# A pre-norm transformer block on one core: one tile's statistics on ScalarE, softmax sums of two units in groups of four, and a new instruction order

## The chip, the core and the metric

The kernel runs on one core of one Trainium2 chip. The metric is the device time of one execution in microseconds, the median of three runs. The engines are named as the profile names them: PE (TensorE matmuls, with its weight loads as PEld), ACT (ScalarE), DVE (VectorE), POOL (GpSimd) and SP (the queue that issues the DMAs).

## The reference

One transformer block over 2048 tokens with 1024 channels, 32 heads of 32 channels and an inner FFN width of 3584, all tensors in bf16. There is no causal mask. The layer norms have no learned scale.

```
h  = x + attention(layernorm(x)) @ wo      # qkv = layernorm(x) @ wqkv, softmax(q k / sqrt(32)) v
h2 = h + gelu(layernorm(h) @ w1 + b1) @ w2 + b2     # gelu in its tanh form
```

## The kernel before

The 2048 tokens are cut into 16 tiles of 128 rows, or into 8 units of 256 queries. The 32 heads form 8 groups (`G`) of 4 heads; the four heads of a group use the four 32-row or 32-column strips of the PE array at once. A *job* is one unit and one group, written (unit, group); there are 64 jobs. A job has 8 *rounds*, and a round covers 256 keys.

A round of a job goes through these steps. `Att.qk` makes eight matmuls of scores on PE (line 1017) into two pairs of PSUM banks. Two ACT instructions of 1024 columns (line 1029) take the exponential and write it into a slot of the ring `PT` (nine rounds; while the lead runs, fourteen further slots named `PX`). `Job.pv` (line 1075) multiplies with V, and into the same bank, beside the result, `Job.den` (line 1115) adds the softmax's row sums with a matrix of ones. To make those sums cheaper for PE, DVE first adds pairs of blocks within a round (line 1092) into one of three `PS` buffers, and for units 0 to 5 adds two such results (line 1098) before `den` takes them; `direct` rounds skip DVE and go from `PT` to `den`. In a normal job round 7 is direct, rounds 0 to 5 are added in three groups of two, and round 6 stands by itself. In the first three jobs, (0,0), (1,0) and (2,0), all rounds are direct. `Job.finish` turns the sums into reciprocals on DVE and writes the normalised output `OT`.

PSUM banks 0 to 5 hold scores. Banks 6 and 7 are shared: a job's result takes one of them, and all background matmuls (projections, output projection `wo`, `ffn1`, `ffn2`) take the other, or whichever is free. A `Slot` is a claim on one of the two.

The work is staged as follows. The *lead* loads x, normalises tiles pair by pair (`lead_norm`, `layer_norm`), transposes each tile on PE (`tr_tile`, `transposes`; line 847 for tiles 0 and 1), copies it to `xnT`, and makes keys and queries of group 0 (`proj_half`) and V (`proj_v1`), so that the first exponentials can start early. `LEAD_ACT` names the tiles whose transposed copy ACT makes; DVE makes the others. A layer norm consists of two half statistics per tile (`half_stats`, line 746), an average (line 755), a conversion `mvb` (759), `tb` (760) and `mvr` (766), a power on POOL (767), a reciprocal (769) and the normalisation itself (772). The remaining projections follow as background work beside the jobs in the order of `ORDER`: (3,0), then groups 1 to 4, then groups 5 to 7, of units 0 and 1 (units 2 and 3 too for group 1). For units 2 and later, the queries are made as background work by `late_q` and pass through DRAM. From then on a unit's output projection, second layer norm and FFN are background work beside the exponentials of later units. Between the exponentials ACT computes the tanh of the gelu (line 1294). The last unit's FFN is the tail.

No instruction order is written by hand. The kernel's text builds a graph of tasks, and `Graph.schedule` plans it with a model of each engine's cost, choosing by priority. The result is five fixed queues, one for each engine. `PRIO_SHIFT` adds a correction to the priority of single tasks and `GROUP_SHIFT` to the place of groups of background matmuls. `PV_BEGIN` and `PV_MUST` say, for each job, at how many waiting rounds `pv` may begin and must run. While the planned time is below `LEAD_HOLD`, DVE may stay idle for a moment when a task with a better priority is about to become ready. `fill_gaps` puts small matmuls without a use (line 1566) into planned gaps of PE in the lead, between 9 and 52 us. The planner's `dma` sizes are costs, not bytes: the factors 2.7 and 3.9 only make the model's transfers longer.

Of the kernel before, what the change touches and what calls it, by code (L numbers as in the profile page):

```python
# [14 lines left out]
LEAD_HOLD = 12.0  # L15
# [52 lines left out]
class Graph:  # L68
# [267 lines left out]
    def emit(self, e, obj):  # L336
# [10 lines left out]
PV_BEGIN = "6776776766675567666685766867867747778757674686786668888633466636"  # L347
PV_MUST = "3743746633366637646276643332732244443446233432453524324325757663"
GROUP_SHIFT = (
        "0:94 1:-298 2:244 3:378 4:-5 5:90 7:79 11:-10 13:-14 15:41 16:-152 17:-8 18:115 19:-291 22:-138 "  # L350
        "25:-30 26:-23 27:-3 28:13 29:-4 34:-8 35:-139 38:16 39:136 40:60 42:2 44:-33 45:90 47:28 52:25 "
        "53:-212 55:-117 56:-80 57:-18 58:25 65:75 67:-10 68:-25 69:295 75:-177 76:-84 78:-19 85:160 86:90 "
        "87:-61 88:-205 89:-62 90:-416 91:-111 95:28 96:49 97:13 98:38 101:598 102:138 103:-16 106:-6 "
        "108:-15 114:-115 115:-169 117:-1 118:-114 119:22 120:-11 122:-107 123:280 125:65 126:-136 127:-18 "
        "128:-5 129:13 130:-12 135:28 136:-30 138:-1 143:1 144:-3 145:11 152:-33 153:-84 155:39 157:-26 "
        "158:-22 162:-30 163:-14 164:-1 165:6 168:-18 170:-24 171:-16 172:50 173:23 174:27 175:45 178:-26 "
        "179:156 180:32 181:-144 188:186 189:4 190:-165 192:-13 193:-61 194:192 195:-16 196:-17 197:-25 "
        "198:-4 199:-219 200:185 203:97 204:-306 205:-31 206:-17 207:48 208:361 218:110 219:-26 220:13 "
        "221:159 222:157 223:361 225:139 226:-173 227:3 233:-18 235:-12 239:-88 248:-125 250:19 251:-159 "
        "253:-3 254:-45 259:-2 261:-24 262:-184 263:-41 268:16 278:-28 280:-84 281:6 283:82 284:79 285:551 "  # L360
        "286:-39 288:-29 289:-87 291:-294 292:274 294:-11 295:83 296:-16 298:246 299:62 310:50 312:14 "
        "315:-100 316:-14 319:7 321:74 322:-18 324:-34 325:-12 326:-214 329:-148 331:-205 332:-18 333:24 "
        "335:57 337:-94 ")
PRIO_SHIFT = (
        "0:-1 2:-2 3:-4 5:2 6:-2 7:-1 8:-15 9:-5 10:-1 13:-1 16:-1 17:4 53:-1 54:-2 57:-1 58:-1 59:2 62:-1 "
        "63:5 65:1 86:-1 87:1 121:2 122:-1 123:-1 124:-1 126:2 129:2 131:-1 132:-3 134:1 143:1 153:-2 154:-2 "
        "183:-3 185:1 186:1 187:-1 189:-1 191:-2 194:-7 195:-1 196:1 216:2 219:-3 222:3 224:-2 225:-1 252:2 "
        "253:1 254:-3 255:4 258:1 259:-4 260:1 261:1 262:-2 263:1 273:1 283:1 288:3 290:-1 293:1 294:5 317:2 "
        "318:-1 319:-1 321:1 322:-1 326:1 327:1 328:1 339:2 350:1 351:2 356:-1 357:-6 374:-2 378:-1 381:1 "
        "382:-1 383:1 384:1 385:2 386:-1 396:1 411:1 412:1 415:3 432:1 433:-1 434:-1 435:2 440:8 441:-2 "  # L370
        "443:-1 454:-1 465:-4 466:-1 469:3 471:-2 472:-1 489:1 495:1 497:-5 498:1 499:1 500:2 501:-2 511:2 "
        "521:-1 529:-1 547:-2 549:-1 550:2 552:-1 579:-2 596:-8 613:2 630:1 647:-2 681:1 715:1 716:-1 717:1 "
        "718:-1 719:-1 721:-2 722:-1 741:3 761:-1 765:1 766:-3 768:-1 769:1 773:-1 774:2 777:-1 780:-2 781:1 "
        "783:-1 785:-3 786:-2 788:-2 789:1 794:1 797:3 799:-1 800:1 803:-1 808:1 817:1 818:2 820:-3 824:1 "
        "827:1 834:1 835:-1 844:6 871:-1 880:-3 922:-1 955:-1 988:-1 1038:-3 1055:3 1072:-1 1092:2 1094:-2 "
        "1095:-1 1099:-2 1100:-1 1102:-2 1103:1 1105:1 1106:1 1109:-1 1118:1 1123:-1 1124:2 1127:1 1129:-2 "
        "1130:-2 1138:-2 1140:-1 1143:-9 1144:1 1146:-2 1155:2 1157:-4 1161:-1 1163:-4 1169:-3 1175:-2 "
        "1176:-2 1179:-2 1182:2 1185:1 1190:-6 1191:-1 1192:-4 1193:-2 1199:2 1201:3 1203:-1 1204:1 1206:-2 "
        "1207:-1 1209:-2 1210:2 1215:1 1216:2 1218:-2 1221:-2 1222:1 1225:1 1227:-1 1228:1 1230:-1 1233:1 "
        "1234:2 1237:-1 1245:-1 1250:-4 1258:-3 1259:-1 1262:1 1267:-1 1268:1 1270:1 1271:-2 1273:-2 1289:-1 "  # L380
        "1306:-1 1315:-3 1324:-2 1359:3 1420:-1 1424:1 1482:-1 1490:-1 1491:3 1494:-1 1496:-1 1499:1 1500:-1 "
        "1510:-1 1511:-1 1541:-2 1593:2 1630:3 1632:-1 1633:2 1635:2 1638:2 1640:-3 1644:1 1647:1 1649:-2 "
        "1650:-1 1652:-1 1659:-2 1661:-3 1664:1 1671:-2 1675:-1 1677:1 1678:-1 1687:-1 1689:-1 1693:2 "
        "1695:-1 1696:-1 1704:3 1705:1 1707:-6 1708:-4 1711:1 1714:2 1716:-1 1719:1 1720:1 1727:-2 1730:-1 "
        "1731:-1 1740:-1 1776:1 1810:1 1846:-2 1852:-1 1855:6 1857:-1 1861:1 1864:-1 1869:2 1876:-2 1878:2 "
        "1879:5 1882:4 1884:-6 1885:-5 1888:1 1892:2 1893:1 1894:-1 1895:-2 1896:-2 1898:-2 1906:-1 1910:2 "
        "1921:1 1928:3 1931:2 1933:-2 1940:1 1944:-1 1945:1 1947:-1 1948:-1 1966:-1 1975:-2 1984:1 2027:-1 "
        "2063:-1 2066:-1 2067:1 2071:-1 2072:-1 2074:2 2075:2 2077:-2 2081:1 2083:-1 2087:1 2089:-2 2090:1 "
        "2095:-1 2096:1 2101:-1 2105:1 2111:1 2112:2 2122:2 2131:1 2140:2 2149:-1 2209:-1 2231:4 2234:1 "
        "2236:-1 2240:5 2242:1 2243:1 2246:-1 2248:-1 2252:-1 2254:-1 2258:-1 2260:-2 2263:2 2264:-1 2266:2 "  # L390
        "2267:2 2270:4 2275:1 2276:3 2278:-2 2287:-1 2314:1 2325:1 2326:4 2328:-1 2329:-1 2334:1 2336:-1 "
        "2345:2 2346:3 2348:1 2349:1 2351:1 2352:3 2355:1 2360:2 2361:-3 2363:1 2364:1 2371:1 2373:-2 2374:7 "
        "2375:-2 2377:-2 2378:-1 2381:1 2385:-2 2388:2 2391:-1 2395:-1 2397:-1 2400:-1 2412:3 2416:1 2419:-1 "
        "2424:1 2425:-3 2426:-1 2427:1 2429:-2 2430:-1 2432:-3 2433:1 2440:-2 2443:-1 2444:3 2447:2 2449:-1 "
        "2452:1 2453:1 2456:1 2464:-1 2465:3 2471:2 2477:1 2478:2 2484:-1 2485:1 2492:-1 2493:1 2499:1 "
        "2504:1 2505:1 2513:-1 2516:-1 2520:1 2523:1 2527:1 2531:1 2533:2 2554:1 2555:1 2565:-1 2575:3 "
        "2577:-1 2587:-2 2596:3 2597:-3 2599:2 2601:-1 2611:-1 2620:-1 2621:1 2639:1 2642:-1 2648:-1 2649:-1 "
        "2651:-2 2653:-1 2654:-1 2655:-1 2661:3 2662:-1 2674:-1 2683:1 2684:1 2695:1 2725:-1 2736:1 2746:1 "
        "2747:-1 2748:1 2765:1 2766:1 2784:1 2787:1 2788:-2 2790:-1 2807:-2 2832:1 2869:1 2871:-1 2872:-1 "
        "2912:-1 2954:-3 2955:1 2975:-1 2976:1 2994:-1 3040:1 3041:-1 3042:-1 3044:1 3045:1 3047:-1 3048:-1 "  # L400
        "3053:1 3056:-1 3059:2 3064:-1 3067:1 3068:-2 3074:1 3076:2 3077:3 3079:-1 3086:-1 3087:1 3089:1 "
        "3094:-2 3095:-2 3100:-1 3101:1 3106:1 3108:1 3115:-2 3130:-1 3140:1 3177:1 3180:-1 3183:1 3196:1 "
        "3203:-1 3206:1 3207:1 3209:1 3212:4 3215:2 3227:-1 3229:-2 3235:1 3236:-1 3238:-1 3245:-1 3249:2 "
        "3253:-2 3254:1 3255:-1 3256:1 3260:3 3264:-1 3271:1 3274:1 3276:-2 3279:-2 3283:1 3292:-2 3299:-1 "
        "3301:-1 3306:-1 3307:2 3309:1 3315:-1 3317:-1 3318:-1 3323:1 3324:1 3330:1 3333:-2 3335:-4 3336:1 "
        "3339:1 3341:-1 3342:-1 3344:-2 3356:-2 3361:-1 3364:3 3373:-2 3392:-4 3401:-4 3403:3 3404:-1 "
        "3405:-2 3406:1 3407:-2 3408:1 3410:1 3413:1 3414:-2 3415:-3 3416:1 3417:1 3418:4 3419:1 3422:1 "
        "3423:-1 3425:1 3426:2 3489:-2 3490:1 3497:-2 3526:3 3527:-4 3556:-1 3557:-1 3575:1 3593:-1 3594:1 "
        "3595:1 3600:1 3637:-5 3639:1 3640:-1 3642:1 3681:2 3683:3 3684:-1 3701:-1 3702:1 3721:-1 3722:3 "
        "3726:1 3761:-1 3762:1 3763:-1 3768:-1 3803:-1 3804:-2 3805:2 3807:-2 3808:-2 3809:1 3845:1 3846:-2 "  # L410
        "3849:1 3850:1 3851:1 3852:-1 3853:1 3863:-1 3873:3 3874:-1 3875:2 3885:-2 3895:1 3896:1 3915:-4 "
# [65 lines left out]
def build_kernel(nc, A_x, A_wqkv, A_wo, B_w1, B_b1, B_w2, B_b2, out):  # L477
# [267 lines left out]
    def half_stats(i, c, src, B_src, prio):  # L745
        return dve(lambda v: v.bn_stats(st_l[:, i, 6 * c:6 * c + 6], src), 0.6, reads=[B_src], writes=[B_stl[i][c]], prio=prio)

    def layer_norm(tiles, prio, norm="dve", quick=True, at=None):

        n = len(tiles)  # L750
        i = ln_slots(n) if at is None else at
# [902 lines left out]
```

## Time and profile before

| | us |
|---|---|
| median of three runs (1068.94 to 1070.45) | 1069.12 |
| the profiled execution | 1069.67 |
| its span, first to last instruction | 1067.9 |
| first exponential starts | 15.37 |
| last exponential ends | 1007.87 |
| PE busy | 1041.4 |
| ACT busy | 1010.0 |
| DVE busy | 837.0 |

The page gives each engine's busy time as a share of the span. The view of windows gives the same for any stretch of the span, so that a stage can be read by itself. The view of waits names what an engine waited for, and the chain of waits follows the last instruction back. The timeline lists instructions in order of time, with the idle time before an instruction in square brackets and what ended it. An exponential of 1024 columns is shown with 1.03 us alone, but follows the one before after about 0.92 us, since their ends overlap. The granted PE clock was 1.00 in nearly all of the span.

### The profile page before, as it was taken

The page shows a single profiled execution, that of the slowest core. Times are in us where ns is not written, and L with a number is a line of the kernel's source. Part 1 is how long each engine was busy: PE and PEld are TensorE (multiplying, and loading weights), DVE is VectorE, ACT ScalarE, POOL GpSimd, SP SyncE. Part 2 cuts the span into 40 slices and gives each one's busy share as a digit, 9 for nine tenths or more (in the row PEclk, how much of TensorE's full clock was granted, in tenths as well). Part 3 has the DMA queues.
Part 4 walks back from the last instruction along what each step waited for, and adds up shares of the span by engine and source line. Part 5 has one row for each costly group of instructions (what it writes and reads, how often), then busy time and mean ns, then how long its engine had stood idle before and what let it go on. Part 6 is the DMA issues. An engine that isn't in the chain of part 4 may idle for free.

```text
span 1067.9 us, 39400 instructions
## 1 busy us (share of the span) xinstructions
PE 1041.4 (98%) x17738; PEld 598.2 (56%) x17738; DVE 837.0 (78%) x1648; ACT 1010.0 (95%) x1118; POOL 18.2 (2%) x34
## 2 busy tenths in 40 slices
PE   8999999999999999999999999999999999899998
PEld 6756555654447546644565466446546744474483
DVE  8757777777888997998799989978887876797511
ACT  5999999999999999999999999999999999999850
POOL 1100000000000000000000000000000000000000
PEclk9999999999999999999999999999999999999999
DMA  7920012005568588647776686577667756887640
GB/s 211 267 50 3 2 42 62 2 2 160 182 164 245 154 199 258 182 148 222 211 219 176 175 254 192 161 243 212 179 173 225 216 172 211 229 236 245 191 150 21
DMA packets 280136, 177.40 MB, mean 166 GB/s; under 512 B 41632, under 2 KB 274848, under 8 KB 279584
## 3 DMA queue, kind: packets, MB, share of 16 engines
q1 hardware_dynamic: 279968, 174.89, 56.5%
q8 instruction: 139, 2.28, 0.9%
q14 instruction: 29, 0.24, 0.1%
HBM read 160.96 MB, written 10.22 MB: 160 GB/s over the span
## 4 chain that ended last, share of the span: by engine, by line
ACT 73%; PE 22%; DMA 3%; DVE 2%; issue 0%; SPq 0%; DVEq 0%
ACT PT L1029 67%; PE ps L698 7%; PE ps L701 5%; ACT tg L1294 4%; PE ps L695 3%; PE ps L1017 3%; PE ps L1075 2%; ACT PX L1029 2%; PE ps L1115 1%; DMA b1b<-in_B_b_dram 1%; DMA a_w1r<-in_B_w_dram 1%; DMA a_w2r<-in_B_w_dram 1%; DMA hnT<-a_xb 1%; DVE PS L1092 0%; DMA xrb<-in_A_x_dram 0%
## 5 line engine op out<-in xcount | busy, mean ns | idle before, releaser
L1029 ACT ACTIVATE PT<-ps 128x1024 bf16<-128x1024 f32 x996 | 928.0, 1201 | 4.7 <-PE ps L1017 4.5
L1092 DVE TENSOR_TENSOR PS<-PT 128x1024 bf16<-128x1024 bf16 x425 | 286.3, 685 | 90.0 <-ACT PT L1029 50.2
L1017 PE MATMUL ps<-QT,KT 32*128 32x256 bf16 x4096 | 204.3, 273 | 9.3 <-ACT PT L1029 5.5
L1075 PE MATMUL ps<-PT,V 128*32 128x256 bf16 x3984 | 162.8, 274 | 0.1
L1017 PEld LDWEIGHTS ps<-QT,KT 32*128 32x128 bf16 x4096 | 60.9, 92 | 171.8 <-ACT PT L1029 161.7
L698 PE MATMUL ps<-hnT,a_w1r 128*128 128x256 bf16 x1161 | 144.0, 273 | 2.7 <-DVE tg L1293 0.8
L698 PE MATMUL ps<-a_w2r,gT 128*128 128x512 bf16 x538 | 132.3, 380 | 0.3
L698 PEld LDWEIGHTS ps<-hnT,a_w1r 128*128 128x128 bf16 x1161 | 105.7, 98 | 35.2 <-issue 18.6
L1075 PEld LDWEIGHTS ps<-PT,V 128*32 128x32 bf16 x3984 | 101.2, 97 | 31.7 <-issue 9.1
L1098 DVE TENSOR_TENSOR PS<-PS 128x1024 bf16<-128x1024 bf16 x135 | 92.4, 685 | 2.2
L1115 PE MATMUL ps<-PS,ones 128*32 128x256 bf16 x1160 | 80.6, 275 | 0.6 <-DVE PS L1092 0.3
L698 PEld LDWEIGHTS ps<-a_w2r,gT 128*128 128x128 bf16 x538 | 46.7, 98 | 61.4 <-issue 15.8
L1271 DVE TENSOR_TENSOR gT<-ps,b1f 128x512 bf16<-128x512 f32 x98 | 66.9, 685 | 17.3 <-PE ps L698 9.6
L695 PE MATMUL ps<-a_w2r,gT 128*32 128x512 bf16 x984 | 72.7, 381 | 0.9 <-DMA a_w2r<-in_B_w_dram 0.8
L1294 ACT ACTIVATE tg<-tg 128x1024 bf16<-128x1024 bf16 x49 | 58.7, 1226 | 0.0
L695 PE MATMUL ps<-hnT,a_w1r 128*32 128x256 bf16 x1628 | 57.9, 274 | 0.1
L695 PEld LDWEIGHTS ps<-hnT,a_w1r 128*32 128x32 bf16 x1628 | 40.7, 96 | 9.3 <-issue 7.4
L698 PE MATMUL ps<-a_w1r,OT 128*128 128x512 bf16 x168 | 41.9, 380 | 1.5 <-issue 0.8
L698 PE MATMUL ps<-xnT,Wall 128*128 128x512 bf16 (+1 forms) x170 | 40.8, 366 | 0.2 <-DVE QT L879 0.2
L698 PE MATMUL ps<-Wall,xnT 128*128 128x256 bf16 x302 | 39.8, 274 | 0.1
L1115 PEld LDWEIGHTS ps<-PS,ones 128*32 128x32 bf16 x1160 | 31.2, 97 | 15.0 <-issue 5.7
L695 PE MATMUL ps<-xnT,Wall 128*32 128x512 bf16 x568 | 39.4, 381 | 0.0
(105 smaller groups left out, 985.2 us busy)
## 6 DMA issues: line engine op xcount, KB each, us to landing
a_w2r<-in_B_w_dram SPq DMA_DIRECT2D x105, 512.0 KB, 4.9
a_w1r<-in_B_w_dram SPq DMA_DIRECT2D x98, 512.0 KB, 4.7
a_w1r<-in_A_wo_dram SPq DMA_DIRECT2D x32, 512.0 KB, 4.6
b_w1r<-in_B_w_dram SPq DMA_DIRECT2D x14, 512.0 KB, 5.1
a_w1r<-in_A_wqkv_dram SPq DMA_DIRECT2D x11, 512.0 KB, 4.3
Wall<-in_A_wqkv_dram SPq DMA_DIRECT2D x16, 256.0 KB, 4.9
hch<-in_A_x_dram SPq DMA_DIRECT2D x16, 256.0 KB, 4.7
xrb<-in_A_x_dram SPq DMA_DIRECT2D x14, 256.0 KB, 4.4
```

The source lines that it names most:

```text
L695: fns.append(lambda p, j=j: p.matmul(psum[32 * j:32 * j + 32, bi(bank), c0:c1], lhsT[:, 32 * j:32 * j + 32], rhs, start=start, stop=stop, ...
L698: t.whole = lambda p: p.matmul(psum[:, bi(bank), c0:c1], lhsT, rhs, start=start, stop=stop, skip_group_check=True)
L701: t = pe(lambda p: p.matmul(psum[:, bi(bank), c0:c1], lhsT, rhs, start=start, stop=stop), occ, reads=reads, writes=[bb(bank)], mode="full" ...
L1017: return p.matmul(psum[:, 2 * us[h // 2] + h % 2, n * i:n * i + n], KT[32 * h:32 * h + 32, g, k0:k0 + P], QT[32 * h:32 * h + 32, qs, 0:n], ...
L1029: x = act(lambda a, u=u, k=k: a.activation(pt(s)[:, k, :, :], psum[:, 2 * u:2 * u + 2, :], ACT.Exp, bias=0.0, scale=SCALE), 1024, reads=[B ...
L1075: fns.append(lambda p, i=i, h=h: p.matmul(psum[32 * h:32 * h + 32, bi(bank), 0:nq], V[:, g, nk * r + i, 32 * h:32 * h + 32], pt(s)[:, h // ...
L1092: dve(lambda v: v.tensor_tensor(PS[:, n, :, :], pairs[:, :, 0:256], pairs[:, :, 256:512], ALU.add), c_dve(1024, 2), reads=[B_PT[2 * s], B_ ...
L1098: dve(lambda v: v.tensor_tensor(PS[:, n, :, :], PS[:, n, :, :], PS[:, m, :, :], ALU.add), c_dve(1024, 2), reads=[B_PS[n], B_PS[m]], writes ...
L1115: fns.append(lambda p, h=h, rhs=rhs, i=i: p.matmul(psum[32 * h:32 * h + 32, bi(bank), nq:2 * nq], ones32[:, :], rhs, start=False, stop=las ...
L1271: drop(dve(lambda v: v.tensor_tensor(gT[:, fc:fc + 2, cs], psum[:, bi(bank), 0:2 * n].rearrange("p (f c) -> p f c", f=2), b1f[:, fc:fc + 2 ...
L1294: act(lambda a: a.activation(t, t, ACT.Tanh, bias=0.0, scale=math.sqrt(2.0 / math.pi)), c, reads=B_t, writes=B_t, prio=-1)
```

## The change

Three things change together. First, in the lead, tile 2's mean and variance come from two ACT instructions with an accumulated sum (a copy, and a square with the negated mean as bias) and two small DVE instructions, in place of two half statistics and an average on DVE. Tile 3's transposed copy and the first query copy go from ACT to DVE; x of tile 3 is loaded ahead of the first weights; V's copy of group 0 gets a better priority; and the hold reaches to 48 us. Second, in the jobs of units 0 and 1 for groups 1 to 7 (14 jobs), all eight rounds go through DVE in two groups of four, and none is direct. Other jobs keep their form. Third, all four tables of the order are replaced, and `fill_gaps` sees the score banks as free from their first use on instead of from 20 us on.

```
-LEAD_HOLD = 12.0
+LEAD_HOLD = 48.0
...
-PV_BEGIN = "6776776766675567666685766867867747778757674686786668888633466636"
-PV_MUST = "3743746633366637646276643332732244443446233432453524324325757663"
+PV_BEGIN = "7466868666566663766578667587867347887757875567678767876564886785"
+PV_MUST = "6553264375657772234355742223743664642632354443335522323335343233"
...
+    def act_stats(j, x_ap, B_x, o_ap, B_o, prio):
+        act(lambda a: a.activation(o_ap, x_ap, ACT.Copy, accum_out=st_l[:, j, 0:1]), 1024,
+            reads=B_x, writes=[B_o, B_stl[j][0]], prio=-3)
+        dve(lambda v: v.tensor_scalar(mv_l[:, j, 0:1], st_l[:, j, 0:1], 1.0 / D, None, ALU.mult), 0.08,
+            reads=[B_stl[j][0]], writes=[B_mv[j]], prio=prio - 6)
+        act(lambda a: a.activation(o_ap, x_ap, ACT.Square, bias=mv_l[:, j, 0:1], scale=-1.0, accum_out=st_l[:, j, 6:7]), 1024,
+            ap_bias=True, reads=B_x + [B_mv[j]], writes=[B_o, B_stl[j][1]], prio=-3)
+        dve(lambda v: v.tensor_scalar(mv_l[:, j, 1:2], st_l[:, j, 6:7], 1.0 / D, None, ALU.mult), 0.08,
+            reads=[B_stl[j][1]], writes=[B_mv[j]], prio=prio)
...
         for k, (x_ap, B_x, o_ap, B_o) in enumerate(tiles):
+            if k in by_act:
+                act_stats(i + k, x_ap, B_x, o_ap, B_o, prio)
+                continue
...
-    LEAD_ACT = [0, 2, 3]
+    LEAD_ACT = [0,2]
     LEAD_DMA = 16
+    STAT_ACT = [2]
...
-                    reads=[bb(bank)], writes=wr, prio=-4 if g == 0 else 0)
+                    reads=[bb(bank)], writes=wr, prio=-21 if g == 0 else 0)
...
-    def QUAD(qb, g):
-        return qb < QA or g < QG
+    def EARLY(qb, g):
+        return g >= 1 and qb < 2
+
+    def SIZE(qb, g):
+        return 4 if EARLY(qb, g) else 2 if qb < QA or g < QG else 1
 
     def DIRECT(qb, g):
-        return 16 if g == 0 and qb < DLEAD else 1
+        return 16 if g == 0 and qb < DLEAD else 0 if EARLY(qb, g) else 1
...
-                if self.half is None and r + 1 < self.nr - self.direct and self.quad:
-                    self.half = n
-                elif self.half is not None:
-                    m, self.half = self.half, None
+                m, self.acc = self.acc, n
+                if m is not None:
                     dve(lambda v: v.tensor_tensor(PS[:, n, :, :], PS[:, n, :, :], PS[:, m, :, :], ALU.add), c_dve(1024, 2),
                         reads=[B_PS[n], B_PS[m]], writes=[B_PS[n]], prio=-2)
+                self.held += 1
+                if self.held == self.size or r + 1 == self.nr - self.direct:
                     self.sums.append((n, False))
-                else:
-                    self.sums.append((n, False))
+                    self.acc, self.held = None, 0
...
-    x_tile(0, -6, 2)
-    x_tile(1, -6, 2)
-    x_tile(2, -5)
-    load_w(WQ, -5, 0, P)
-    load_w(WK, -5, 0, P)
-    for tt in range(3, 8):
-        x_tile(tt, -5)
+    x_tile(0, -9, 2)
+    x_tile(1, -9, 2)
+    x_tile(2, -8)
+    x_tile(3, -8)
+    load_w(WQ, -7, 0, P)
+    load_w(WK, -7, 0, P)
+    for tt in range(4, 8):
+        x_tile(tt, -6)
     load_w(WV, -5, 0, 256)
...
         if hc == 0:
-            proj_half(0, 0, 0, ev)
+            proj_half(0, 0, 0, "dve")
...
-                held.setdefault(2 * u, [(0.0, t1 / 2.6, [])]).append((t.done - t.lat - t.occ, x.done, [x]))
+                held.setdefault(2 * u, [(0.0, x.done - 0.01, [])]).append((t.done - t.lat - t.occ, x.done, [x]))
```

Left out here are the two long tables `GROUP_SHIFT` and `PRIO_SHIFT` (all of their entries are new) and the planner's cost factors for the first transfers.

## The prediction

> **What bounds the kernel now.** First the page's busy shares with the chain of waits, then the windows, because shares average over stages with different limits.
>
> ```profile
> PE 1041.4 (98%) x17738; PEld 598.2 (56%) x17738; DVE 837.0 (78%) x1648; ACT 1010.0 (95%) x1118; POOL 18.2 (2%) x34
> ...
> ACT 73%; PE 22%; DMA 3%; DVE 2%; issue 0%; SPq 0%; DVEq 0%
> ```
>
> PE has the larger share and ACT the longer chain; the windows decide (columns: stretch, length, then busy us and count of PE, PEld, DVE, ACT, POOL; clock, DMA share, GB/s). I cut them at the first exp (15.37) and at the end of the last (1007.87).
>
> ```profile
> 15.37:60.00 44.63, 41.83 (x756) 31.03 (x757) 32.67 (x93) 43.36 (x51) 4.40 (x6) 1.00 0.83 232
> 60.00:100.00 40.00, 39.50 (x910) 25.69 (x902) 28.19 (x55) 39.59 (x44) 0.00 (x0) 1.00 0.01 3
> 100.00:310.00 210.00, 207.84 (x3683) 111.01 (x3679) 165.76 (x307) 209.50 (x230) 1.99 (x2) 1.00 0.25 74
> 250.00:310.00 60.00, 58.57 (x1113) 28.09 (x1101) 50.40 (x99) 60.00 (x67) 1.99 (x2) 1.00 0.66 192
> 1007.87:1015.20 7.33, 7.33 (x54) 3.51 (x54) 6.00 (x23) 2.68 (x5) 0.54 (x1) 1.00 0.98 300
> 1015.20:1067.90 52.70, 49.53 (x393) 33.90 (x391) 5.87 (x12) 15.13 (x31) 0.55 (x1) 0.99 0.26 82
> ```
>
> From first to last exp ACT idles 1.27 (to 60), 0.41 (to 100), 0.50 (to 310) and, in the same view cut further on, 1.39, 0.78, 0.05, 0 and 0.84: 5.24 us of 992.50. The span is thus 15.37 to the first exp, 987.26 of ACT work, 5.24 of ACT idle, and 60.03 behind the last exp, where the last unit's normalisation and FFN follow in a fixed order. PE is full as well, but a faster PE shortens nothing unless ACT was waiting for it; that is at most 5.24 us. So a gain has to come from an earlier first exp, from ACT work removed behind it, or from the 5.24.
>
> The timeline of the lead shows what stands before the first exp (start, duration, engine, line).
>
> ```profile
> 6.22 1.29 DVE L746 BATCH_NORM_STATS2 st<-xrb 128x6 f32<-128x512 bf16 x2
> 7.42 0.15 DVE L759 CAST mvb<-mv 128x4 bf16<-128x4 f32 x1
> ...
> 10.40 1.09 ACT L854 ACTIVATE xnT<-ps 128x512 bf16<-128x512 bf16 x2 [8.39 <-PE ps L847]
> 12.54 0.38 ACT L980 ACTIVATE QT<-ps 128x256 bf16<-128x256 f32 x1 [1.05 <-PE ps L701]
> 13.10 0.38 ACT L980 ACTIVATE KT<-ps 128x256 bf16<-128x256 f32 x1 [0.17 <-PE ps L701]
> 13.54 1.94 ACT L801 ACTIVATE xnT<-ps 128x1024 bf16<-128x1024 bf16 x2
> 15.37 1.03 ACT L1029 ACTIVATE PT<-ps 128x1024 bf16<-128x1024 f32 x1
> ```
>
> Tile 2's statistics sit on DVE between the averages of tiles 0 and 1 and their mvb, which starts the chain to the first normalised tile; ACT is idle 8.39 us meanwhile; and the first exp, whose scores were begun at 13.66, queues behind the two copies of tiles 2 and 3.
>
> **Part 1: the lead.** Tile 2's statistics leave DVE: two halves, 1.29 us, so mvb can start up to 1.3 us sooner. W is no barrier: the K weights were issued near 4.55 and land some 5.1 us later (DMA view), 9.7; K's matmuls start at 12.06 (half of the 2.00 us from 11.06) and would move to 10.8. In the new DMA order Q's weights go one transfer sooner, tile 2 one later: issued at about 2.9 plus 4.4, it lands near 7.3. On ACT come a Copy and a Square over 1024 columns. No such op with a sum is in the trace; the nearest row is the 1024-wide copy, 1.94 for two, so about 1.0 each, with a 0.15 us DVE op between and another behind (as mvb and tb). Bounds: 0.9 (an exp's spacing, 3.77 for four) and 1.4 (should the sum need another small op, like the smallest ACT copy, 0.38). They run about 7.3 to 9.5, inside ACT's idle stretch, but tile 0's copy, then wanted at 9.1, waits to 9.5: of the 1.3 us I keep 0.9. ACT loses tile 3's copy in front of the first exp: 0.97. The QT copy leaves ACT at 12.54, where it idled: 0, and on DVE (0.41) it is done before KT is. DVE loses 1.29 and an average (0.21), gains two small ops (0.3), tile 3's copy (0.69) and QT (0.41): 0.1 less, nothing. I subtract 0.2 for those DVE copies queued in front of a step. Sum 0.9 + 0.97 - 0.2 = 1.7: first exp near 13.7. Ends: 2.3 earlier (1.3 + 0.97, ScalarE never late) and 0.3 later (tile 2 lands late; Square holds up tile 0's copy by a full op).
> [...]
>
> Will ACT be fed? From 13.7 it has eight exps (0.92 each) and copies of 1.26: to 22.3. The third step's scores were ready only for the exp at 24.17, so they must come 1.9 sooner. DVE ran ten half-statistics from 10.41 to 18.09 before it normalised tiles 4 and 5 at 18.88; only four of those ten (2.5 us) belong to them. The longer hold (48 instead of 12 us) lets the planner prefer that chain, and V's copy (0.40) at the front costs little. I count the 1.7 as kept; the other end is all of it lost as ACT idle. Fill matmuls placed in more banks: 12 took 0.84 at 19.12, ahead of scores for which ACT idled 0.50; taken at nothing, 0.5 either way.
>
> **Part 2: the 14 jobs of units 0 and 1, groups 1 to 7.** Per job the sums' matmuls go from four groups of four and one direct set of eight to two groups of four.
>
> ```profile
> 138.89 0.40 PE L1075 MATMUL ps<-PT,V 128*32 128x256 bf16 x8
> 139.12 0.28 PE L1115 MATMUL ps<-PS,ones 128*32 128x256 bf16 x4
> 139.23 0.39 PE L1115 MATMUL ps<-PT,ones 128*32 128x256 bf16 x8
> ```
>
> Starts give 0.11 for four and 0.23 for eight: 0.67 becomes 0.22, 14 x 0.45 = 6.3 us of PE. DVE goes from seven pair adds and three second adds to eight and six: four more at 0.685, 2.74 a job, 38.4 in all (0.60 each back to back: 33.6). PE's 6.3 meets 0.91 us of ACT idle between 60 and 310; it is worth 0 to 0.9 there, and I take 0.4. DVE's 38.4 lies in slack: 128 to 250 it is busy 92.55 of 122, and 8.3 jobs add 22.7: 94%. From 250 to 310, 4.1 jobs add 11.2 to 50.40: 61.6 of 60. That is the tight place, a shortfall of 1.6, or 3.4 at the 97% that DVE reached in 550 to 600 (48.44 of 50, ACT idle 0.06). PE being up to 6 us ahead moves evictions forward, and nine rounds of PT cover some late adds; taken at nothing, at worst 5 (below). The last round's add and its second add now stand between the last exp and the closing sum: up to 1.4 us more per job in which one of the two shared banks is held. Other background work and the next PV queue behind that on PE; 14 x 0.45 saved pays for about a third, the rest eats PE slack, not ACT.
>
> **Part 3: the order.** The tables are new and cannot be priced by line. What they can win is the ACT idle behind 310, 3.06 us, part of it behind PE, which now has 6.3 us less to do; I take 0.5. What they can lose is bounded by the worst stretch: 1.39 idle in 90 us (310 to 400), over 992 us 15.3, that is 10 more; since all other stretches are below 0.011 per us, the value lies near zero. Tail: 60.03, within 0.5.
>
> **Sum.** 1.7 + 0.4 + 0.5 = 2.6 us. The profiled execution took 1069.67 (span 1067.9 and 1.77 around it), 0.55 above the median; 1067.1 would follow for it, with a span near 1065.3, and 1069.12 - 2.6 = 1066.5 for the median. About 0.2% (2.1 us) is what a measurement of this kernel can tell from no change.
>
> **Rivals.** *DVE becomes the bound from 250 on (slower).* For: 61.6 us of adds and evictions in 60. A job there costs DVE 15.1 and in-order waits for PE's sums (33.8 us over 63 jobs, 0.5 each), 15.6 against the 14.7 of its sixteen exps: 0.9 x 4 jobs = 3.7, and up to 1.4 more where the query copies for unit 2 (a_ost) come late: 5.1. It decides once the nine PT rounds are full. In the case where the lead's gain is given up to supply as well, 1069.1 + 5.1 = 1074.2; with it, 1072.5, which I take. Against: windows at 97% elsewhere left ACT fed. 0.19.
> *The lead's gain is lost*, ACT waiting near 22 for the third step: 1069.0. For: DVE is busy 9.8 and 10.0 of 10 us from 10 to 30. 0.12.
> *All the idle goes*: 2.3 + most of the 3.97 behind 60, 1063.4. For: the chain's PE stretches; against: DMA and ACT's own rhythm are part of them. 0.10.
> *Square brings table loads.* The trace has two, at the first Copy and the first gelu, 1.283 each; if Square brought one and the exp another, one falls in the idle and one on the path with a late Square: 1.3 to 2.6 back, 1068.5. For it speaks only that gelu brought one. 0.04.
> [...]
> That the change doesn't do what it says can be read off counts: L1098 from 135 to 177, L1092 from 425 to 439, PS sums (L1115) from 1160 to 1048.
>
> **Numbers.** Forecast 0.55, its own range 1064.8 to 1068.5, of which 0.40 beyond 2.1 us and 0.15 within. Faster: 0.40 + 0.10 = 0.50. Slower: 0.16 of the DVE case, 0.03 of the lost lead, 0.01 of the loads: 0.20. Same: the rest, 0.30. The range leaves out half of the best case and most of the upper part of the DVE case, some 0.17: 1063.5 to 1071.8.
>
> **What would show it.** First exp near 13.7 with one ACT copy in front; ACT idle behind it at or below 5.2; 60 us behind the last exp; DVE near 98% from 250 to 310. Wrong if the first exp is at 15 or later, if ACT idles over 2 us near 22 or between 250 and 320, or if another ACT_TABLE_LOAD stands in the lead.

## The result: slower by 0.3% where 0.2% faster was forecast

The changed kernel took 1073.13 us (median of 16 runs, 1071.16 to 1080.43), the kernel before 1070.28 beside it (16 runs): a ratio of 1.0032, 95% interval 1.0019 to 1.0045. The profiled run took 1073.42, its span 1071.6, 3.7 more than before's 1067.9. The forecast for the median was 1066.5, and 1071.8 the end of its range; 1.16 of the 6.6 us between forecast and result are the base, since the kernel before's median was 1069.12 over three runs and 1070.28 over these 16. Five of the changed kernel's runs had a granted clock of 0.994 or 0.995 and took 1074.48 us or more, the other eleven, at 0.997 or 0.998, have a median of 1072.25, so the clock can be a part of the difference, not all of it.

The page of the changed kernel: busy shares, chain by engine, the groups that the change touches.

```profile
PE 1040.5 (97%) x17687; PEld 594.9 (56%) x17687; DVE 870.1 (81%) x1705; ACT 1011.4 (94%) x1120; POOL 17.7 (2%) x34
...
ACT 68%; PE 26%; DVE 2%; DMA 2%; issue 1%; SPq 0%; POOLq 0%; POOL 0%; DVEq 0%
...
L1101 DVE TENSOR_TENSOR PS<-PT 128x1024 bf16<-128x1024 bf16 x439 | 295.5, 686 | 70.4 <-ACT PT L1035 43.6
...
L1105 DVE TENSOR_TENSOR PS<-PS 128x1024 bf16<-128x1024 bf16 x177 | 121.2, 685 | 2.4
```

The change does what it says: 439 pair adds, 177 second adds. ACT's part of the chain fell from 73% to 68%, and PE's rose from 22% to 26%: ACT waits more. The windows say where (columns as in the prediction).

```profile
14.31:60.00 45.69, 44.87 (x781) 33.89 (x783) 36.91 (x98) 44.17 (x51) 4.13 (x6) 1.00 0.83 223
...
100.00:310.00 210.00, 203.79 (x3520) 106.78 (x3513) 190.56 (x348) 208.95 (x229) 1.54 (x2) 1.00 0.24 73
250.00:310.00 60.00, 55.91 (x898) 25.84 (x897) 57.10 (x112) 60.00 (x67) 1.54 (x2) 1.00 0.62 186
600.00:800.00 200.00, 194.86 (x3439) 109.53 (x3432) 174.54 (x343) 197.52 (x217) 2.99 (x4) 1.00 0.71 204
...
1011.75:1071.60 59.85, 56.17 (x445) 37.02 (x441) 11.87 (x33) 17.85 (x35) 1.52 (x2) 1.00 0.31 101
```

The kernel before, in the stretch that differs most:

```profile
600.00:800.00 200.00, 197.80 (x3396) 110.62 (x3388) 175.27 (x344) 199.95 (x219) 3.39 (x5) 1.00 0.70 200
```

ACT is never idle from 250 to 310, where DVE was feared, and the tail is 59.85 us (60.03 before). ACT idles 2.48 us from 600 to 800 (0.05 before) and, cut in the same way, 2.73 from 400 to 600 (0.78 before). Counting exponentials (1024 in each kernel), the 501st starts 1.18 us earlier than in before's profile, the 551st 0.93 later, the 701st 3.23 later. The largest single idle time of ACT there comes from one stop of PE, seen in the timelines of both; 106 us on PE waits for a weight block as well.

```profile
534.96 0.27 PE L1123 MATMUL ps<-PT,ones 128*32 128x256 bf16 x1
537.11 0.40 PE L1123 MATMUL ps<-PT,ones 128*32 128x256 bf16 x7 [1.88 <-issue]
...
643.18 1.58 PE L690 MATMUL ps<-hnT,a_w1r 128*128 128x256 bf16 x13 [1.94 <-DMA a_w1r<-in_B_w_dram]
```

```profile
537.89 3.77 ACT L1035 ACTIVATE PT<-ps 128x1024 bf16<-128x1024 f32 x4 [1.89 <-PE ps L1023]
```

PE stops between the first and the second of eight like matmuls, with operands at hand ("issue": nothing that the profile shows was waited for), and ACT goes idle for just as long. The DMA view of 534.5 to 536 shows what was on the move: weights, and one packet of queue 8, kind "instruction".

```profile
DMA  9999999999999999999999999997976977877856
...
q1 hardware_dynamic: 844, 0.44, 97.4%
q8 instruction: 1, 0.02, 4.0%
```

The trace holds 139 such packets of 16,384 bytes, one for about every 255 instructions of PE (17,687 matmuls and as many weight loads); that they are PE's own is read from this count. This one started at 534.75 and took 0.95 us; PE went on 1.4 us after it had landed. Below, a *packet stop* is a gap in PE of over 0.45 us between 60 and 1015 us that ends with nothing released and 1.0 to 1.7 us after such a packet has landed. Before's profile has one (0.69 us at 443.54), the changed kernel's two (1.88 and 0.69).

### The profile page after: what moved, and what is told of

It reads as the page before. It is cut to its first block, busy times and chain, and to the rows that moved or that the text cites. A ratio compares the mean times of both kernels' runs of the same rounds, so it can differ in the third digit from the quotient of the medians.

```text
span 1071.6 us, 39346 instructions
## 1 busy us (share of the span) xinstructions
PE 1040.5 (97%) x17687; PEld 594.9 (56%) x17687; DVE 870.1 (81%) x1705; ACT 1011.4 (94%) x1120; POOL 17.7 (2%) x34
## 4 chain that ended last, share of the span: by engine, by line
ACT 68%; PE 26%; DVE 2%; DMA 2%; issue 1%; SPq 0%; POOLq 0%; POOL 0%; DVEq 0%
ACT PT L1035 63%; PE ps L690 8%; PE ps L693 5%; PE ps L687 5%; PE ps L1023 4%; ACT tg L1302 3%; PE ps L1084 2%; ACT PX L1035 2%; DMA a_w1r<-in_B_w_dram 1%; PE ps L1123 1%; DVE PS L1101 1%; DMA a_w2r<-in_B_w_dram 1%; DMA xrb<-in_A_x_dram 0%; DVE PS L1105 0%; DVE st L738 0%
## 5 line engine op out<-in xcount | busy, mean ns | idle before, releaser
L1101 DVE TENSOR_TENSOR PS<-PT 128x1024 bf16<-128x1024 bf16 x439 | 295.5, 686 | 70.4 <-ACT PT L1035 43.6
L1084 PE MATMUL ps<-PT,V 128*32 128x256 bf16 x3984 | 159.5, 274 | 1.0 <-issue 0.4
L1105 DVE TENSOR_TENSOR PS<-PS 128x1024 bf16<-128x1024 bf16 x177 | 121.2, 685 | 2.4
L690 PE MATMUL ps<-a_w2r,gT 128*128 128x512 bf16 x471 | 116.2, 380 | 0.4 <-DVE a_ost L1331 0.2
L687 PE MATMUL ps<-a_w2r,gT 128*32 128x512 bf16 x1252 | 89.0, 381 | 0.7 <-DMA a_w2r<-in_B_w_dram 0.5
L1123 PE MATMUL ps<-PS,ones 128*32 128x256 bf16 x1048 | 72.8, 276 | 1.5 <-DVE PS L1105 0.8
L690 PEld LDWEIGHTS ps<-a_w2r,gT 128*128 128x128 bf16 x471 | 41.0, 98 | 54.8 <-issue 13.2
L690 PE MATMUL ps<-xnT,Wall 128*128 128x512 bf16 (+1 forms) x192 | 46.5, 367 | 0.2 <-DVE V L948 0.2
L687 PEld LDWEIGHTS ps<-a_w2r,gT 128*32 128x32 bf16 x1252 | 28.1, 96 | 25.4 <-issue 12.2
L1123 PEld LDWEIGHTS ps<-PS,ones 128*32 128x32 bf16 x1048 | 27.9, 97 | 16.3 <-issue 5.9
```

The costliest lines, as they stand in the source:

```text
L687: fns.append(lambda p, j=j: p.matmul(psum[32 * j:32 * j + 32, bi(bank), c0:c1], lhsT[:, 32 * j:32 * j + 32], rhs, start=start, stop=stop, ...
L690: t.whole = lambda p: p.matmul(psum[:, bi(bank), c0:c1], lhsT, rhs, start=start, stop=stop, skip_group_check=True)
L1084: fns.append(lambda p, i=i, h=h: p.matmul(psum[32 * h:32 * h + 32, bi(bank), 0:nq], V[:, g, nk * r + i, 32 * h:32 * h + 32], pt(s)[:, h // ...
L1101: dve(lambda v: v.tensor_tensor(PS[:, n, :, :], pairs[:, :, 0:256], pairs[:, :, 256:512], ALU.add), c_dve(1024, 2), reads=[B_PT[2 * s], B_ ...
L1105: dve(lambda v: v.tensor_tensor(PS[:, n, :, :], PS[:, n, :, :], PS[:, m, :, :], ALU.add), c_dve(1024, 2), reads=[B_PS[n], B_PS[m]], writes ...
L1123: fns.append(lambda p, h=h, rhs=rhs, i=i: p.matmul(psum[32 * h:32 * h + 32, bi(bank), nq:2 * nq], ones32[:, :], rhs, start=False, stop=las ...
```

## Experiments

Ratios are to the kernel before on the same chip, with 95% intervals.

### Splices of the two orders

Four kernels in which each engine's queue is written out in full, taken from the two kernels' plans: up to a planned time from one, behind it from the other. The theory to test was that the new order behind 310 us makes the loss.

```diff
-    t = the ready task with the best priority
+    t = self.tasks[FORCED[e.name][pos[e]]]     # the engine's queue, written out
 # s1: before to 313 us, then the new order
 # s2: lead, groups of four and order of the changed kernel to 320 us, then before's order
 # s3: the new lead to 53 us, then before's sums and order
 # s4: before's lead to 53 us, groups of four and new order to 320, then before's order
```

> All of before up to 313 us of the planned time, with its lead, its sums and its order; behind that the five queues follow the new order. The theory that the loss sits in the new order behind 310 us, where two PE stalls on weight blocks (1.94 and 1.06 us) and one of 1.88 us stand in the changed kernel's trace: 3 to 4 us slower than before, ACT idle behind 310 near 6.5 in place of 3.1. The rival that the extra DVE adds cost it, and the rival that the lead does: no change, within 1 us.

Measured: 1.0018 (1.0009 to 1.0026).

> All of the changed kernel up to 320 us of the planned time, with its lead, its sums in groups of four and its order; behind that the order of before. Theory of the order: no change against before, within 1 us, first exp at 14.3, ACT idle behind 320 near 3. Theory of the DVE adds: 3 us slower, with ACT idle between 100 and 320. Forecast of the prediction for this part (lead 1.7, PE 0.4): 2 us faster.

Measured: 1.0054 (1.0036 to 1.0071).

> The changed lead alone (tile 2's statistics on ACT, its order up to 53 us), with the sums and the order of before behind it. The changed kernel's trace has the 47th exp at 59.97, as before has, so the theory that the lead's gain is given back by 60 us: no change, within 1 us, although the first exp comes 1.1 us sooner. Prediction: 1.7 us faster.

Measured: 1.0035 (1.0021 to 1.0049).

> The sums in groups of four for the 14 jobs with the new order from 53 to 320 us, the lead and the order behind 320 of before. Theory of the order: no change, within 1 us; DVE near 55 to 57 of 60 between 250 and 310. Theory that DVE becomes the bound: 3 us slower, with exps waiting between 250 and 320. Prediction: 0.4 us faster.

Measured: 1.0020 (1.0007 to 1.0033).

The theory fell. Every piece costs something, and the costs don't add up to the whole: the lead alone costs as much as the whole change, and s2, which has the old order behind 320, costs most. Their profiles have packet stops of 3.9, 4.0, 3.8 and 2.5 us, all of them behind 320 us, where s2, s3 and s4 have the order of before, which stopped only once there in its first profile.

### The same program behind 17, 34 or 51 more matmuls

If PE stops where one packet of instructions ends and the next is late, any instruction more at the start moves all borders. (The 256 to a packet in the expectations stands for about 255: the counts give 255.2 matmuls and weight loads to a packet in before and 254.5 in the changed kernel.) The `N_WARM` matmuls, which run before x arrives and whose result nothing uses, were split into narrower ones; order, operands and waits of everything else stay.

```diff
-    for k in range(N_WARM):                    # 34
-        pe(lambda p: p.matmul(psum[:, 3, 0:256], ident[:, :], b2t[:, 0:256], ...), 0.177, ...)
+    WARM = [1, 2] * 17                         # 17 more;  [2] * 34: 34 more;  [2] * 17 + [3] * 17: 51 more
+    for n in WARM:
+        w = 256 // n
+        pe([lambda p, w=w: p.matmul(psum[:, 3, 0:w], ident[:, :], b2t[:, 0:w], ...)] * n, 0.177, ...)
```

> The kernel before, with 17 of the 34 warming matmuls at the start split in two (128 columns each instead of 256), so that TensorE's program is 17 matmuls longer ahead of the first useful instruction, and nothing else: order, operands and waits of all five engines stay. Theory F (TensorE now and then stops for its own next packet of 256 instructions; where the packets' borders fall depends on how many instructions came before): the two stops of before (0.69 us at 443.54 and 0.78 at 576.33) move or vanish and others come, and the time follows the sum of the stops, by -1.5 to +4 us. Rival O (the time is set by the order of the work alone): no change, within 1 us of the kernel before.

> The kernel before with all 34 warming matmuls split in two: 34 matmuls more at the start, nothing else changed. Theory F: between 17 more (+2.7 us) and 51 more (+4.3) nothing can be interpolated; it has its own stops, and its time goes with their sum: base of about 1066.6 plus 0.9 times the sum. Rival O (order alone): no change, within 1 us of before.

> The kernel before, with 17 of the 34 warming matmuls split in two and 17 in three: 51 matmuls more at the start, nothing else changed. Theory F: other stops than in the kernel before and than with 17 more, and a time that follows their sum, -1.5 to +4 us. Rival O: no change, within 1 us.

> The changed kernel with 17 warming matmuls more in the same way. Theory F: its stops inside TensorE's work (1.88 us at 537.11 and 0.69 at 569.71) move or vanish, others come; -2.5 to +3 us beside the changed kernel's +3.4 over the kernel before, with the sum of the stops. Rival O: +3.4 us over the kernel before as it was, within 1 us.

> The changed kernel with 34 matmuls more at the start. Theory F: own stops, a time of -2.5 to +3 us beside the changed kernel. Rival O: as the changed kernel, +3.4 us over before.

> The changed kernel with 51 warming matmuls more. Theory F: stops elsewhere than in the changed kernel, -2.5 to +3 us beside it, with their sum. Rival O: +3.4 us over the kernel before, within 1 us.

The expectations count a gap of 0.78 us near 576 (0.68 in one) as a stop. It returns in every profile of the kernel before, with or without added matmuls, and the last packet had landed 4.8 us or more earlier: it is no packet stop, and the table leaves it out.

| kernel | matmuls added | ratio | packet stops in the profile, us |
|---|---|---|---|
| before | 0 | 1 | 0.69 |
| before | 17 | 1.0026 (1.0016 to 1.0035) | 4.52 |
| before | 34 | 1.0038 (1.0023 to 1.0054) | 2.65 |
| before | 51 | 1.0041 (1.0027 to 1.0056) | 6.71 |
| changed | 0 | 1.0032 (1.0019 to 1.0045) | 2.57 |
| changed | 17 | 1.0018 (1.0006 to 1.0031) | 0 |
| changed | 34 | 1.0024 (1.0007 to 1.0041) | 2.71 |
| changed | 51 | 1.0010 (0.9996 to 1.0024) | 0.75 |

Splitting some matmuls that do nothing useful costs the kernel before as much as the whole change does. The order alone (rival O) would have left every row of a kernel alike, and for before the three intervals rule that out; the changed kernel's rows overlap, so for it a shift with the alignment is not shown by the times. Over four alignments before averages 1.0026 and the changed kernel 1.0021, which these intervals can't tell apart: the comparison of the two as they stand mostly compares before's best alignment of four with what looks like the changed kernel's worst. As far as four alignments tell, that before had the better one is luck and not a merit of its order.

The stops lie at fixed counts of matmuls, whatever stands there. Matmul 12,580 (the one with 12,580 ahead of it) is the first behind a stop in before with 17, 34 and 51 more: a score matmul, a row sum and a PV matmul in turn. The counts lie whole packets apart: with 51 more there are stops at 9,401 and 12,580, 25 times 127.2 matmuls with their weight loads. The largest stop of all, in before with 51 more, is there:

```profile
724.05 0.28 PE L1075 MATMUL ps<-PT,V 128*32 128x256 bf16 x4
727.26 0.37 PE L1075 MATMUL ps<-PT,V 128*32 128x256 bf16 x4 [2.93 <-issue]
```

The times don't follow the stops of one profile alone: the changed kernel with 17 more has none, but a stop of 1.58 us at 924.32 of another kind, whose cause stays open, and 2.7 us of waits for w2 blocks. Nor is a long stop over with its own length. Behind the 2.93 us the view of windows gives a granted PE clock of 0.51 from 727.3 to 730.7 (four row sums take 0.22 us there, from 728.01 to the next start, and 0.11 at 723.94); the two other packet stops of over 2 us (2.05 and 2.04, in s4 with 34 and 51 more, below) have such a stretch of 3.4 us at half clock from 928.2 and 730.0, 0.6 and 0.1 us behind them. None of the shorter ones, up to 1.88 us, brought one of its own; each profile has one that starts between 911 and 925 (3.4 us from 917.0 in before's, 6.8 from 918.8 in the changed kernel's), where PE waits for ACT twice within 4 us, 1.2 to 1.4 us each.

### Both kernels once more

> The kernel before once more, unchanged, for a second profile. Theory F (the stops for TensorE's packets of instructions belong to the program): stops at the same two instructions, near 443.5 us (0.69 before) and 576.3 us (0.78), and none over 0.45 us elsewhere between 60 and 1015 us. Rival C (the stops are chance, another set in every execution): other places, at a sum anywhere from 1 to 7 us.

> The changed kernel once more, unchanged. Theory F: stops at the same two instructions, near 537.1 us (1.88) and 569.7 us (0.69). Rival C: other places and another sum. The waits of TensorE for a weight block at 643.2 us (1.94) and 743.4 us (1.06): there again within 0.5 us if the order of the loads makes them; gone or elsewhere if they are one execution's contention.

Both theories were half right. The second profile of before stops at the same matmul near 444 (0.69) and at matmul 12,580 as well (0.85), where the first had none. The changed kernel stops at the same matmul near 537 again, but for 0.71 instead of 1.88, and at three other borders, 4.20 in all. So in these four profiles the program fixes where PE can stop; whether it does, and for how long, differs from run to run. The two waits for w1 blocks at 643 and 743 were gone: they belong to one execution, not to the new order.

### A quarter of the weight bytes

What makes a packet late, weight traffic or something in PE's own program? In these kernels each block after a slot's first is loaded for a quarter only (the rest of the slot keeps old weights, so the results are not the block's). Instructions and waits are the same.

```diff
 def wblock(R, src_ap, prio=1):                 # wo, wqkv, w1
-    dma(R.w1[s][:, :, :], src_ap.rearrange("(dc p) c -> p dc c", p=P), ...)
+    n = 2 if (R, "w1", s) in full else DC      # DC = 8; w2 blocks: 1 of 4
+    full.add((R, "w1", s))
+    dma(R.w1[s][:, 0:n, :], src_ap.rearrange("(dc p) c -> p dc c", p=P)[:, 0:n, :], ...)
```

> The kernel before with 51 matmuls more (four tenths of a per cent slower than before, eight stops of 7.49 us in its profile), with each weight block after a slot's first loaded for a quarter only: of wo, wqkv and w1 blocks two of eight chunks, of w2 blocks one of four; the rest of the slot keeps old weights. Same instructions, same waits. Theory D (a packet of instructions comes late because it is held up by weight traffic): at a quarter of the bytes the stops shrink to under 1.5 us in sum, TensorE's waits for blocks vanish, and the time falls to about 1.000 of before or under. Rival P (the packet is asked for late for a reason in TensorE's own program, such as many short matmuls since the last): the stops stay at 4 us or more at the same counts (matmul 12580 and its like), and the time stays over 1.002.

Measured: 0.9966 (0.9954 to 0.9978), down from 1.0041. No packet stop is left; of the sum of stops that was expected to stay under 1.5 us, the 0.78 us near 574 is all there is. At the border of the 2.93 us PE now runs on but for some 0.15 us (eight matmuls in 0.54 us, 0.39 or 0.40 for eight alike before it), and in 719.5 to 722 the DMA engines are nearly idle:

```profile
720.18 0.28 PE L1115 MATMUL ps<-PS,ones 128*32 128x256 bf16 x4
720.29 0.54 PE L1075 MATMUL ps<-PT,V 128*32 128x256 bf16 x8
```

```profile
DMA  4100100000000000000000000000000000000000
```

In 723.5 to 726 of the same program with full loads it was the opposite:

```profile
DMA  9999999999999999999999999997875421131121
...
q8 instruction: 1, 0.02, 2.6%
```

Weight traffic it is (theory D). The packets are not slower on their way: behind 320 us they take 0.96 us in the median with full loads in before with 51 more, 1.08 with quarter loads. So the delay lies ahead of their first byte. The packet of this border starts 2.11 us before its first PV matmul with quarter loads (718.18 and 720.29), and 0.70 us after it with full loads (724.75 and 724.05). An estimate for all packets behind 320 us sets each one's start against the exponentials begun by then, at 0.97 us each: with full loads they start 0.7 us later in the median and over 2 us later in one of ten; between the two profiles of before as it is, the median is 0.02. What holds the packets ahead of their first byte no trace shows; what the runs show is that the stops go with the bytes of the other queue (at this border q1 filled 85.6% of the engines' time with full loads, 2.0% with quarter loads).

The last pair measures the change with the traffic taken out, both kernels as they stand:

> The kernel before as it is (no matmuls added), each weight block after a slot's first loaded for a quarter only (wo, wqkv, w1: two of eight chunks; w2: one of four). Theory D (the stops and the waits for blocks come from weight traffic): as light_51, 0.9966 of before within 0.001, although the alignment differs by 51 matmuls, and no stop for a packet. Rival P: the alignments still differ, by 0.2% or more.

> The changed kernel with the same quarter loads: what the change is worth when nothing waits for weight traffic. If the forecast's sum holds there (lead 1.7, groups of four 0.4, order 0.5): 2.6 us under light_before, 0.994 of before. If the lead's gain is lost by the 47th exponential and the order's with it: within 1 us of light_before, 0.996 to 0.9975. If the change's own order costs 3 us (its idle time is its own and not the traffic's): 0.999 to 1.000.

Measured: 0.9973 (0.9958 to 0.9988) and 0.9971 (0.9955 to 0.9986), medians 1067.44 and 1067.36. That is the second of the three cases. Without the traffic the change shows no gain: 0.08 us where 2.6 were forecast. Each ratio has an interval of 1.6 us each way; beside each other, the twelve runs of each leave -0.7 to +0.8 us (an estimate, from resampling them). Traffic costs the kernel before 0.27% and the changed kernel 0.61% (1.0032 to 0.9971): the whole difference between the two, as far as the intervals tell. The windows from 320 to 1000 us, for the kernel before and the changed one, then for both with quarter loads, show ACT idle for 3.06, 6.48, 0.97 and 1.03 us:

```profile
320.00:1000.00 680.00, 665.98 (x11552) 374.94 (x11550) 575.78 (x1111) 676.94 (x737) 7.62 (x12) 1.00 0.71 204
320.00:1000.00 680.00, 664.22 (x11618) 372.98 (x11616) 572.48 (x1107) 673.52 (x733) 7.33 (x12) 0.99 0.70 203
320.00:1000.00 680.00, 663.49 (x11531) 375.92 (x11573) 577.09 (x1113) 679.03 (x741) 8.14 (x12) 0.99 0.28 79
320.00:1000.00 680.00, 664.55 (x11716) 376.23 (x11752) 578.72 (x1119) 678.97 (x741) 7.33 (x12) 1.00 0.29 79
```

No packet stop is in either profile with quarter loads, and before with 51 more and before as it is differ by 0.0007 instead of 0.0041.

### The early part of the change, at three more alignments

s4 had the least span without its stops. Would another alignment make it faster than both kernels?

> s4 (lead of before, groups of four and the new order to 320 us, order of before behind) with 17 warming matmuls more. s4 itself was at 1.0020 with 2.52 us of stops in its profile, 1064.4 us of span without them, the lowest of all. Theory F: the time follows the stops of this alignment; averaged over four alignments s4 is 1 to 2 us below the kernel before averaged over its four (1.0026), so 1.001 to 1.002. Rival O (s4's parts cost what they cost): 1.0020 in all.

> s4 with 34 matmuls more. Theory F: its own stops; with under 1 us of them it would be at 0.998 to 1.000 of before and beat both kernels. Rival O: 1.0020.

> s4 with 51 matmuls more. Theory F: its own stops; with under 1 us of them 0.998 to 1.000 of before. Rival O: 1.0020.

Measured: 1.0030 (1.0014 to 1.0047), 1.0044 (1.0032 to 1.0056) and 1.0094 (1.0079 to 1.0109), with packet stops of 3.72, 8.72 and 7.34 us: again the time does not go with the stops of one profile, and ACT waits 16.4 us in the last one, so more than half of that has other sources. Averaged over four alignments s4 is at 1.0047, above both kernels, not below before as expected. That its early part is worth 1 to 2 us was read off single profiles, and it fell. No version here that loads all its weights beat the kernel before.

## Why the prediction was wrong, by its steps

Two steps failed. The terms 1.7, 0.4 and 0.5 were counted as gains that reach the end, and of their 2.6 us the pair with quarter loads shows 0.08. And no term stood for weight traffic, which costs the changed kernel 0.34% more than the kernel before at these alignments.

**The lead's 1.7 us, counted as kept.** The first exponential did come near 13.7 (14.31 here; 14.0 on average over the eight profiles with the new lead, against 15.5 over the twelve with the old). By the third the gain is gone: 18.0 on average against 17.8. The timelines of DVE and ACT show how; in the kernel before the second and third were one group:

```profile
16.80 1.99 ACT L1029 ACTIVATE PT<-ps 128x1024 bf16<-128x1024 f32 x2
```

The changed kernel:

```profile
6.58 0.69 DVE L738 BATCH_NORM_STATS2 st<-xrb 128x6 f32<-128x512 bf16 x1 [1.08 <-DMA xrb<-in_A_x_dram]
7.19 0.26 DVE L760 BATCH_NORM_AGGREGATE mv<-st 128x2 f32<-128x12 f32 x2
7.49 0.17 DVE L764 CAST mvb<-mv 128x4 bf16<-128x4 f32 x1
```

```profile
7.22 1.06 ACT L741 ACTIVATE xb<-xrb 128x1024 bf16<-128x1024 bf16 x1 [5.20 <-DMA xrb<-in_A_x_dram]
8.18 0.19 ACT L741 ACTIVATION_READ_ACCUMULATOR xb<-xrb 128x1 f32 x1
8.61 1.15 ACT L745 ACTIVATE xb<-xrb,mv 128x1024 bf16<-128x1024 bf16 x1 [0.25 <-DVE mv L743]
9.67 0.19 ACT L745 ACTIVATION_READ_ACCUMULATOR xb<-xrb,mv 128x1 f32 x1
...
14.31 1.02 ACT L1035 ACTIVATE PT<-ps 128x1024 bf16<-128x1024 f32 x1 [0.59 <-PE ps L1023]
15.23 1.02 ACT L806 ACTIVATE xnT<-ps 128x1024 bf16<-128x1024 bf16 x1
16.14 0.39 ACT L963 ACTIVATE V<-ps 128x256 bf16<-128x256 f32 x1
16.40 1.04 ACT L1035 ACTIVATE PT<-ps 128x1024 bf16<-128x1024 f32 x1
17.41 0.38 ACT L986 ACTIVATE KT<-ps 128x256 bf16<-128x256 f32 x1
18.30 1.02 ACT L1035 ACTIVATE PT<-ps 128x1024 bf16<-128x1024 f32 x1 [0.51 <-PE ps L1023]
```

Two of its parts failed. The 0.9 us for an earlier mvb: it starts at 7.49 (7.42 before), since in the place of tile 2's statistics a half statistic of tile 3 stands in DVE's queue ahead of the averages, and it waited 1.08 us for its x. How long it waits differs from run to run (mvb starts at 6.56 to 7.49 in the eight profiles, 7.09 on average, and at 7.51 on average in the twelve), so some 0.4 of the 0.9 came. And the copies: tile 3's did leave ACT (0.97, as said), but the first exponential came sooner mostly because tile 2's copy no longer stood in front of it. It stands right behind it and ends at 16.25; PE's next projections start at 16.31, keys follow at 17.41, scores at 17.85, and the third exponential at 18.30, after 0.51 us of waiting. The prediction's own sign, "one ACT copy in front", failed: there was none. This is its rival "the lead's gain is lost", met at 18.3 us instead of 22. (The 1069.0 that the prediction gives for that rival is not its own sum: without the 1.7 the other two terms leave 1068.2.) Of the ops themselves the price was right: 1.06 and 1.15, and 0.19 for each sum, in ACT's idle time. No table load came with Square: the trace's two start at 0.73 and 1022.06 (0.73 and 1018.45 in before), 1.283 us each.

**Groups of four (0.4) and the order (0.5).** From the third exponential on, the two kernels with quarter loads show ACT idle (gaps over 0.25 us) for 3.19 us in before and 3.07 in the changed one: 0.12 gained where 0.9 was counted. The seven waits of before, 0.30 to 0.63 us each, were replaced by six of 0.5 us, all for scores as well, the last four at 219.67, 240.44, 501.64 and 928.24. The DVE rival, priced at up to 5.1, was false: DVE is busy 57.10 of 60 us from 250 to 310, not 61.6, and ACT did not idle there.

**What the sum lacked.** It took the ACT idle of one profile as the kernel's own. Of the kernel before, 0.27% is traffic, and of the changed kernel 0.61%: packet stops and waits for blocks, which no term of the sum held. The bound of 10 us for a worse order was wide enough for it, but the value was put near zero because the stretches of before looked even. They looked even at one alignment. Why traffic hurts one alignment more than another, and why each of the three with more matmuls is worse for before, was only counted, not derived.

## What to carry to other kernels

When a change with a sound price comes out a few tenths of a per cent wrong, run the old and the new kernel with a few harmless instructions added at the start before explaining it by the change: if that moves the time as much, the comparison is of alignments, and only their average, or a run with the disturbing traffic taken out, says what the change is worth. A gap marked "issue" in the middle of like matmuls, with a packet of kind "instruction" landing just before its end (1.0 to 1.7 us here), is the sign. And an earlier first instruction is a gain only as far as the third and the tenth come earlier too: follow what was moved from in front of it to behind it.

## Hardware behaviour that was not expected

- In both kernels 139 packets of kind "instruction", 16,384 bytes each, land while the kernel runs (queue 8; in before's profile they start from 16.5 to 1044.7 us), one for about every 255 matmuls and weight loads of PE; that they are PE's own is an estimate from this count. PE's packet stops end 1.0 to 1.7 us after one has landed and take 0.5 to 2.9 us; behind each of the three of over 2 us (2.93, 2.05, 2.04) the granted PE clock was half for 3.4 us.
- The stops go with weight traffic: with 204 GB/s moved from 320 to 1000 us (before) there were one to seven in each profile of before, at every alignment, with 79 GB/s (quarter loads; 78 with 51 more) none in three profiles.
- Each of the two ACT instructions with an accumulated sum (1.06 and 1.15 us) was followed by a read of the accumulator of 0.19 us.
